# Routing steps with lower bound and step width side by side in one tile, one summing instruction and two moving instructions per step

## The chip, the cores and the metric

The kernel runs on one core of one Trainium2 chip. Its metric is device time in microseconds (us). Five engines work side by side, each through its own queue in order: PE (TensorE, matmuls; PEld is its weight load), DVE (VectorE), ACT (ScalarE), POOL (GpSimd) and SP, which here only issues DMAs. They wait for one another through semaphores. SBUF is the working memory, PSUM holds eight banks into which matmuls write.

## What is computed

The reference chains three blocks: attention over a local band and block summaries, a dense feed-forward block with a gate, and a mixture of eight experts in which every token goes to exactly one expert. The third is the one that matters here:

```python
def _moe2_ref(x, w_gate, w1, w2):
    N, D = x.shape                      # 1536, 512
    E = w_gate.shape[1]                 # 8
    cap = N // E                        # 192
    logits = x @ w_gate
    order = np.argsort(-logits.flatten())
    assigned = -np.ones(N); counts = np.zeros(E)
    for idx in order:
        tok, e = idx // E, idx % E
        if assigned[tok] >= 0 or counts[e] >= cap:
            continue
        assigned[tok] = e; counts[e] += 1
    for e in range(E):
        mask = assigned == e
        out[mask] = np.maximum(x[mask] @ w1[e], 0.0) @ w2[e]
```

The greedy loop means: each expert has a lower bound on the logit that it still takes, and the eight bounds have to be such that each expert ends with exactly 192 tokens.

## The kernel before

Attention and the first product of the feed-forward block (`gemm1`) come first, then the second product (`gemm2`), then the experts. Between `gemm1` and the experts the tokens have to be assigned. The kernel does this while `gemm2` runs: the function `drive` takes the two generators (`second`, which is `gemm2`, and `routing`) and interleaves them by fixed weights, so that the order of instructions on each queue is settled when the program is written. On PE this gives, per routing step, one batch of 12 small matmuls of the routing (L894) and then 18 matmuls of `gemm2` (L704 to L706), and then the next batch.

`route` finds the eight bounds in 15 steps (and a 16th that only makes the assignment). Logits of all tokens lie as 128 partitions x 12 x 8. The bounds `lo` and step widths `step` are 8 numbers each, the same on all partitions. One step does this on DVE, unless PE is named:

- L870 to L882: which logits are below the bound, each token's best expert among those left (`prop`), and beside these small instructions on 8 columns: L873 and L874 make 1/`step`, L878 makes `lo - step`.
- L885, L887, L889: for each token the number of step widths by which its logit lies above the bound, and the comparison of it with 16 thresholds at once (`C`, 128 x 1536 in 16 bits; in the profile its name is `big`).
- L894, on PE: 12 matmuls with a matrix of ones count the tokens per expert and threshold into PSUM.
- L897, L899: the count is compared with the capacity, and each hit is multiplied by a table entry (`dG` for the bound, `dU` for the width); L901 and L903 sum each of these over the 16 thresholds.
- L904, L906: the bound moves by sum times `step`; L908: the width becomes (1 + sum) times `step`.

`lo` lies in SBUF. `step`, its successor `step2`, the product `inc`, the logits' copy `Lp`, `Lm` and `u` lie in one PSUM bank (`state`). The semaphore waits among DVE's own instructions go by whole tiles: one that reads this bank waits for the last one that wrote it, whichever part that was.

During the steps ACT and POOL prepare operands for `gemm2`: ACT rounds a slice (L681), POOL forms the remainder (L682, both inputs and the output in SBUF); they do two slices per routing step, and their start is set by the `gemm2` matmuls on PE that release their buffers.

Of the kernel before, what the change touches and what calls it, by code (L numbers as in the profile page):

```python
# [7 lines left out]
FT = mybir.dt.float32  # L8
# [4 lines left out]
OP = mybir.AluOpType  # L13
AX = mybir.AxisListType
# [8 lines left out]
E, EF = 8, 1024  # L23
N = B * S
CAP = N // E
NT = N // 128
# [14 lines left out]
J = 16  # L41
# [41 lines left out]
def attention_moe_moe(tc, q, k, v, w_in, w_out, w_gate, w1, w2, out):  # L83
    with ExitStack() as ctx:
        build(ctx, tc, q, k, v, w_in, w_out, w_gate, w1, w2, out)


def build(ctx, tc, q, k, v, w_in, w_out, w_gate, w1, w2, out):
    nc = tc.nc
    PE, ACT, DVE, POOL, SP = nc.tensor, nc.scalar, nc.vector, nc.gpsimd, nc.sync  # L90
# [28 lines left out]
    def bank(i):  # L119
        return psum.tile([128, 512], FT, name=f"bank{i}")  # L120
# [658 lines left out]
    for u in range(NU):  # L779
# [5 lines left out]
        else:  # L785
# [4 lines left out]
            big = late.tile([128, 2 * 2 * 512], I32)  # L790
# [16 lines left out]
    def last_sums():  # L807
        while taken[0] < NF:
            out_slice()
            yield 2000  # L810
        for g in range(NF // FG, NF // FG + 2):
            fold_pair(g)
            yield 900
        routing_constants()
        for u in range(NU):
            yield from logits(u)
        summed.append(1)
# [1 line left out]

    prop = late.tile([128, NT, E], F16)  # L820
    jc, C = [big[:, i * 768:(i + 1) * 768].bitcast(F16).rearrange("p (j c) -> p j c", j=J) for i in range(2)]
    dG, dU = [big[:, 1536 + i * E * J:1536 + (i + 1) * E * J].bitcast(FT).rearrange("p (e j) -> p e j", e=E)
              for i in range(2)]
    ones = big[:, 1792:1792 + 64].bitcast(F16)
    g = [0.0] + [RATIO ** i for i in range(J - 1)]
    upd = [1.0] + [(b - a) / g[-1] * SPREAD for a, b in zip(g, g[1:])] + [GROW]

    def routing_constants():
        POOL.memset(ones, 1.0)
        for j in range(J):  # L830
            DVE.memset(jc[:, j, :], 0.5 if j == 0 else g[j] + 1.0)
            DVE.memset(dG[:, :, j], 0.0 if j == 0 else g[j] - g[j - 1])
            DVE.memset(dU[:, :, j], upd[j + 1] - upd[j])

    okf = late.tile([128, 1], FT)
    slot = late.tile([128, NT], I32)
# [1 line left out]
    def small(name, shape, dt=FT):  # L838
        return late.tile(shape, dt, name=name, bufs=2)

    def bc(x):
        return x[:, None, :].to_broadcast([128, NT, E])

    def route():
        mm = small("mm", [128, 2, E])
        Le = L.rearrange("p t e -> p e t")
        DVE.tensor_reduce(mm[:, 0], Le, axis=AX.X, op=OP.max)
        DVE.tensor_reduce(mm[:, 1], Le, axis=AX.X, op=OP.min)
        DVE.tensor_scalar(mm[:, 1], mm[:, 1], -1.0, None, op0=OP.mult)
        yield 100  # L850
        p = bank(7)
        PE.transpose(p[:2 * E, :128], mm.rearrange("p a e -> p (a e)"), ident)
        mc = small("mc", [2 * E, 1])
        DVE.tensor_reduce(mc, p[:2 * E, :128], axis=AX.X, op=OP.max)
        yield 100
        p = bank(7)
        PE.matmul(p[:, :2 * E], mc.to_broadcast([2 * E, 128]), ident[:2 * E, :2 * E], start=True, stop=True)
        state = bank(4)
        Lp, Lm, u = [state[:, i * NT * E:(i + 1) * NT * E].rearrange("p (t e) -> p t e", t=NT) for i in range(3)]
        step, inc, step2 = [state[:, 3 * NT * E + i * E:3 * NT * E + (i + 1) * E] for i in range(3)]  # L860
        DVE.tensor_copy(Lp, L)
        lo = small("lo", [128, E])
        DVE.tensor_scalar(lo, p[:, E:2 * E], -1.0, None, op0=OP.mult)
        DVE.tensor_tensor(step, p[:, :E], lo, op=OP.subtract)
        DVE.tensor_scalar(step, step, 1.0 / g[-1], 1e-30, op0=OP.mult, op1=OP.max)
        for n in range(STEPS):
            last = n == STEPS - 1
            below = small("Lm", [128, NT, E])
            pm = small("pm", [128, NT])
            DVE.tensor_tensor(below, Lp, bc(lo), op=OP.is_lt)  # L870
            if not last:
                inv = small("inv", [128, E])
                DVE.tensor_scalar(inv, step, 1e-30, None, op0=OP.max)  # L873
                DVE.reciprocal(inv, inv)  # L874
            DVE.scalar_tensor_tensor(Lm, below, -BIG, Lp, op0=OP.mult, op1=OP.add)
            if not last:
                l1 = small("l1", [128, E])
                DVE.tensor_tensor(l1, lo, step, op=OP.subtract)  # L878
            DVE.tensor_reduce(pm, Lm, axis=AX.X, op=OP.max)
            if not last:  # L880
                DVE.tensor_tensor(u, Lp, bc(l1), op=OP.subtract)
            DVE.tensor_tensor(prop, Lm, pm[:, :, None].to_broadcast([128, NT, E]), op=OP.is_equal)  # L882
            if last:
                return
            DVE.scalar_tensor_tensor(u, u, 0.0, bc(inv), op0=OP.max, op1=OP.mult)  # L885
            w = small("w", [128, NT * E], F16)
            DVE.scalar_tensor_tensor(w, u.rearrange("p t e -> p (t e)"), 6e4, prop.rearrange("p t e -> p (t e)"),  # L887
                                     op0=OP.min, op1=OP.mult)
            DVE.tensor_tensor(C, w[:, None, :].to_broadcast([128, J, NT * E]), jc, op=OP.is_ge)  # L889
            yield 100  # L890
            p = bank(7)
            Cv = C.rearrange("p j (t e) -> p j t e", e=E)
            for t in range(NT):
                PE.matmul(p[:, :J * E], ones, Cv[:, :, t, :], start=t == 0, stop=t == NT - 1)  # L894
            cnt = p[:, :J * E].rearrange("p (j e) -> p e j", e=E)
            ge = small("ge", [128, E, J])
            DVE.scalar_tensor_tensor(ge, cnt, CAP - 0.5, dG, op0=OP.is_ge, op1=OP.mult)  # L897
            gu = small("gu", [128, E, J])
            DVE.scalar_tensor_tensor(gu, cnt, CAP - 0.5, dU, op0=OP.is_ge, op1=OP.mult)  # L899
            gain = small("inc", [128, E])  # L900
            DVE.tensor_reduce(gain, ge, axis=AX.X, op=OP.add)  # L901
            up = small("up", [128, E])
            DVE.tensor_reduce(up, gu, axis=AX.X, op=OP.add)  # L903
            DVE.tensor_tensor(inc, gain, step, op=OP.mult)  # L904
            lo2 = small("lo", [128, E])
            DVE.tensor_tensor(lo2, lo, inc, op=OP.add)  # L906
            lo = lo2
            DVE.scalar_tensor_tensor(step2, up, 1.0, step, op0=OP.add, op1=OP.mult)  # L908
            step, step2 = step2, step

    tok = late.tile([128, NT], FT)
    POOL.iota(tok, pattern=[[128, NT]], base=0, channel_multiplier=1, allow_small_or_imprecise_dtypes=True)
# [32 lines left out]
    def routing():  # L945
        while not summed:
            yield 50
        yield from route()
        yield 100
        place(prop, True)  # L950
        placed[0] = 1
        POOL.iota(at, pattern=[[1, CAP]], base=0, channel_multiplier=0, allow_small_or_imprecise_dtypes=True)
        DVE.tensor_copy(lslot, slot[:, NT - 1:])
        DVE.tensor_scalar(hot, at, lslot, None, op0=OP.is_equal)
# [267 lines left out]
```

## Time and profile before

| | us |
|---|---|
| median of 3 runs | 597.47 (595.98 to 600.57) |
| the profiled execution, its own time | 597.21 |
| its span, first to last instruction | 595.4 |
| PE busy | 554.4 (93%) |
| DVE busy | 384.4 (65%) |
| ACT busy | 288.7 (48%) |
| POOL busy | 170.2 (29%) |

The mean granted TensorE clock is 0.971 of full speed. The busy share is an average over stages: attention and `gemm1` fill the first 296 us, the routing steps lie between 307 and 394 us beside `gemm2`, and the experts run from 430 us on. The part of the page that cuts the span in 40 slices shows PE at eight to nine tenths in the slices of the routing steps.

### The profile page before, as it was taken

The numbers are of one execution on the slowest core, as the hardware profiler recorded it, in microseconds if no ns is written. First come the engines' busy times: TensorE is split into PE (matmuls) and PEld (weight loads), VectorE is DVE, ScalarE is ACT, GpSimd is POOL, SyncE is SP. The second block draws the span as 40 slices with busy tenths as digits, with TensorE's granted clock in tenths as the row PEclk, the third lists the DMA queues.
The fourth block names the chain that finished last, engine by engine and source line by source line (L and its number), as shares of the span: only waits on it lengthen the run. The fifth ranks groups of instructions, "written<-read, shape, count | busy, mean of one in ns | idle before, by whom it ended". The sixth has DMA issues, their size and how long they took to land.

```text
span 595.4 us, 10943 instructions
## 1 busy us (share of the span) xinstructions
PE 554.4 (93%) x3811; PEld 469.4 (79%) x3811; DVE 384.4 (65%) x1215; ACT 288.7 (48%) x694; POOL 170.2 (29%) x204
## 2 busy tenths in 40 slices
PE   7769889989999999999999899899999999999994
PEld 6647778878899989976677667678789888988883
DVE  6787985655534397731037787762588888888880
ACT  4265654435645445651131131133577777776760
POOL 1424448211111024562243344445101101110011
PEclk9688899989999999999999999999999999999997
DMA  9974991202220245420070000003579878878811
GB/s 207 245 193 101 236 275 35 53 18 62 52 48 1 70 146 175 143 64 1 1 211 2 0 2 1 0 33 129 175 224 282 238 242 272 270 230 270 246 59 32
DMA packets 102400, 75.06 MB, mean 126 GB/s; under 512 B 47488, under 2 KB 88448, under 8 KB 101952
## 3 DMA queue, kind: packets, MB, share of 16 engines
q1 hardware_dynamic: 100352, 67.96, 41.4%
q0 software_dynamic: 1984, 6.32, 2.9%
q8 instruction: 32, 0.52, 0.4%
q14 instruction: 32, 0.26, 0.2%
HBM read 67.55 MB, written 6.71 MB: 125 GB/s over the span
## 4 chain that ended last, share of the span: by engine, by line
PE 43%; issue 26%; DVE 18%; DMA 5%; POOL 3%; ACT 2%; SPq 1%; POOLq 0%; DVEq 0%; ACTq 0%
PE bank L587 7%; PE bank L588 6%; PE bank L589 6%; PE bank L704 4%; PE bank L705 3%; PE bank L706 3%; DVE big L889 3%; POOL out_dram L1025 2%; PE bank L894 2%; DVE bank L268 2%; PE bank L419 2%; PE bank L613 2%; DMA t<-in_moe_w_in_dram 2%; DMA t<-in_q_dram 2%; PE bank L372 2%
## 5 line engine op out<-in xcount | busy, mean ns | idle before, releaser
L587 PE MATMUL bank<-x,wh 128*128 128x384 f32 x256 | 92.5, 361 | 6.6 <-DVE t L601 5.1
L295 DVE TENSOR_TENSOR wl<-t,wh 128x1024 fp32r<-128x1024 f32 x64 | 77.0, 1220 | 20.5 <-ACT wh L294 18.7
L681 ACT ACTIVATE work<-t 128x384 fp32r<-128x384 f32 (+2 forms) x80 | 36.4, 459 | 106.2 <-PE bank L705 101.9
L588 PE MATMUL bank<-x,wh 128*128 128x384 f32 x256 | 87.0, 340 | 0.6 <-DVE x L77 0.6
L589 PE MATMUL bank<-x,wl 128*128 128x384 f32 x256 | 87.2, 340 | 0.1
L590 ACT ACTIVATE t<-bank,three 128x384 f32<-128x384 f32 x64 | 37.2, 581 | 93.8 <-PE bank L589 93.7
L682 POOL TENSOR_TENSOR tlx<-t,work 128x384 fp32r<-128x384 f32 (+1 forms) x52 | 55.8, 1074 | 83.4 <-ACT work L681 83.4
L704 PE MATMUL bank<-wh,work 128*128 128x512 f32 x192 | 78.1, 407 | 0.0
L706 PE MATMUL bank<-wh,tlx 128*128 128x512 f32 x192 | 75.3, 392 | 0.1
L705 PE MATMUL bank<-wl,work 128*128 128x512 f32 x192 | 74.8, 390 | 0.0
L1050 PE MATMUL bank<-x,wh 128*128 128x384 f32 x256 | 73.7, 360 | 0.5 <-DVE x L976 0.5
L294 ACT ACTIVATE wh<-t 128x1024 fp32r<-128x1024 f32 x64 | 65.6, 1048 | 0.0
L1052 PE MATMUL bank<-x,wl 128*128 128x192 f32 x256 | 64.2, 251 | 0.0
L601 DVE SCALAR_TENSOR_TENSOR t<-t,bank 128x384 f32<-128x384 f32 x64 | 34.9, 549 | 39.7 <-ACT t L590 39.6
L396 POOL TENSOR_TENSOR A<-A,sm 128x480 f32<-128x480 f32 x24 | 23.7, 987 | 124.2 <-ACT at L406 72.6
L587 PEld LDWEIGHTS bank<-x,wh 128*128 128x128 f32 x256 | 48.7, 190 | 11.5 <-DVE t L601 4.3
L1025 POOL DMA_INDIRECT out_dram<-t,idx x16 | 14.9, 929 | 141.6 <-DVE t L1074 136.1
L588 PEld LDWEIGHTS bank<-x,wh 128*128 128x128 f32 x256 | 48.9, 191 | 1.2 <-DVE x L77 1.1
L589 PEld LDWEIGHTS bank<-x,wl 128*128 128x128 f32 x256 | 48.8, 191 | 0.5 <-POOL wl L286 0.5
L1052 PEld LDWEIGHTS bank<-x,wl 128*128 128x128 f32 x256 | 48.9, 191 | 0.3
L1066 PE MATMUL bank<-wh,t 128*128 128x512 f32 x128 | 49.0, 392 | 0.0
L1050 PEld LDWEIGHTS bank<-x,wh 128*128 128x128 f32 x256 | 48.0, 188 | 1.2 <-DVE x L976 0.8
(184 smaller groups left out, 1072.0 us busy)
## 6 DMA issues: line engine op xcount, KB each, us to landing
t<-in_moe_w_dram SPq DMA_DIRECT2D x128, 256.0 KB
t<-in_moe_w_in_dram SPq DMA_DIRECT2D x16, 512.0 KB
big<-in_moe_w_out_dram SPq DMA_DIRECT2D x16, 512.0 KB
VW<-in_v_dram SPq DMA_DIRECT2D x20, 192.0 KB
t<-in_v_dram SPq DMA_DIRECT2D x4, 768.0 KB
t<-xs SPq DMA_DIRECT2D x8, 258.0 KB
raw<-in_q_dram SPq DMA_DIRECT2D x8, 256.0 KB
t<-in_k_dram SPq DMA_DIRECT2D x12, 128.0 KB
```

The costliest lines, as they stand in the source:

```text
L294: ACT.activation(hi, x, AF.Copy)
L295: DVE.tensor_tensor(lo, x, hi.bitcast(FT), op=OP.subtract)
L587: PE.matmul(p, wh[:, kk, :], xh[:, kk, :], start=kk == 0, stop=False)
L588: PE.matmul(p, wh[:, kk, :], xl[:, kk, :], start=False, stop=False)
L589: PE.matmul(p, wl[:, kk, :], xh[:, kk, :], start=False, stop=kk == KD - 1)
L682: (DVE if placed[0] else POOL).tensor_tensor(ths[i][1], t, ths[i][0].bitcast(FT), op=OP.subtract)
L704: PE.matmul(acc[j], th[:, c], WH[s], start=f == 0, stop=False)
L705: PE.matmul(acc[j], th[:, c], WL[s], start=False, stop=False)
L706: PE.matmul(acc[j], tl[:, c], WH[s], start=False, stop=f == NF - 1)
L1050: PE.matmul(p, a[:, kk, :], xt[:, kk].rearrange("p c s -> p (c s)"), start=kk == 0, stop=False, skip_group_check=True)
L1052: PE.matmul(p[:, :CAP], b[:, kk, :], xt[:, kk, 0, :], start=False, stop=kk == KD - 1, skip_group_check=True)
L1066: PE.matmul(p, x, w, start=m == 0 and i == 0, stop=m == NM - 1 and i == 2)
```

## The change

`lo` and `step` become the two halves of one SBUF tile `ls` (128 x 2 x 8). The tables `dG` and `dU` become one table `dGU`, the two sets of hits one tile `hit` (128 x 2 x 8 x 16). Both comparisons stay, but one TENSOR_REDUCE sums both sets (128 x 256 to 128 x 16, into the PSUM bank), one multiplication by `step` makes both moves and one addition makes the new pair of bound and width. So L901 and L903 become one instruction, and L904, L906, L908 become two; a step has 16 DVE instructions where it had 18.

```diff
-    dG, dU = [big[:, 1536 + i * E * J:1536 + (i + 1) * E * J].bitcast(FT).rearrange("p (e j) -> p e j", e=E)
-              for i in range(2)]
+    dGU = big[:, 1536:1536 + 2 * E * J].bitcast(FT).rearrange("p (a e j) -> p a e j", a=2, e=E)
...
-        step, inc, step2 = [state[:, 3 * NT * E + i * E:3 * NT * E + (i + 1) * E] for i in range(3)]
+        gains, moves = [state[:, 3 * NT * E + i * 2 * E:3 * NT * E + (i + 1) * 2 * E].rearrange("p (a e) -> p a e", a=2)
+                        for i in range(2)]
         DVE.tensor_copy(Lp, L)
-        lo = small("lo", [128, E])
+        ls = small("lo", [128, 2, E])
+        lo, step = ls[:, 0], ls[:, 1]
...
-            ge = small("ge", [128, E, J])
-            DVE.scalar_tensor_tensor(ge, cnt, CAP - 0.5, dG, op0=OP.is_ge, op1=OP.mult)
-            gu = small("gu", [128, E, J])
-            DVE.scalar_tensor_tensor(gu, cnt, CAP - 0.5, dU, op0=OP.is_ge, op1=OP.mult)
-            gain = small("inc", [128, E])
-            DVE.tensor_reduce(gain, ge, axis=AX.X, op=OP.add)
-            up = small("up", [128, E])
-            DVE.tensor_reduce(up, gu, axis=AX.X, op=OP.add)
-            DVE.tensor_tensor(inc, gain, step, op=OP.mult)
-            lo2 = small("lo", [128, E])
-            DVE.tensor_tensor(lo2, lo, inc, op=OP.add)
-            lo = lo2
-            DVE.scalar_tensor_tensor(step2, up, 1.0, step, op0=OP.add, op1=OP.mult)
-            step, step2 = step2, step
+            hit = small("ge", [128, 2, E, J])
+            for i in range(2):
+                DVE.scalar_tensor_tensor(hit[:, i], cnt, CAP - 0.5, dGU[:, i], op0=OP.is_ge, op1=OP.mult)
+            DVE.tensor_reduce(gains, hit, axis=AX.X, op=OP.add)
+            DVE.tensor_tensor(moves, gains, step[:, None].to_broadcast([128, 2, E]), op=OP.mult)
+            ls2 = small("lo", [128, 2, E])
+            DVE.tensor_tensor(ls2, moves, ls, op=OP.add)
+            ls, lo, step = ls2, ls2[:, 0], ls2[:, 1]
```

With the shorter text all later lines of `route` count otherwise: what is L870 before is L871 after, L873 is L874, L874 is L875, L875 is L876, L878 is L879, L879 is L880, L881 is L882, L889 is L890, L894 is L895.

The end of a step on DVE, before (bank_3296 holds the counts, bank_3250 is `state`, `inc` in the first TENSOR_REDUCE is the tile of `gain`; a bracket says that the instruction waits for an earlier one of DVE or for PE):

```order
L897 SCALAR_TENSOR_TENSOR ge<-bank_3296,big 128x128 [waits PE_49]
L899 SCALAR_TENSOR_TENSOR gu<-bank_3296,big 128x128
L901 TENSOR_REDUCE inc<-ge 128x8 [waits DVE_49]
L903 TENSOR_REDUCE up<-gu 128x8 [waits DVE_49]
L904 TENSOR_TENSOR bank_3250<-inc,bank_3250 128x8 [waits DVE_49]
L906 TENSOR_TENSOR lo<-lo,bank_3250 128x8 [waits DVE_49]
L908 SCALAR_TENSOR_TENSOR bank_3250<-up,bank_3250 128x8 [waits DVE_49]
```

The same place after the change:

```order
L899 SCALAR_TENSOR_TENSOR ge<-bank_3296,big 128x128 [waits PE_49]
L899 SCALAR_TENSOR_TENSOR ge<-bank_3296,big 128x128
L900 TENSOR_REDUCE bank_3250<-ge 128x16 [waits DVE_49]
L901 TENSOR_TENSOR bank_3250<-bank_3250,lo 128x16 [waits DVE_49]
L903 TENSOR_TENSOR lo<-bank_3250,lo 128x16 [waits DVE_49]
```

Two sums and three moves have become one sum and two moves, each of which needs the one just in front of it.

The start of the following step on DVE, before (`l_3328` is `lo - step`):

```order
L870 TENSOR_TENSOR Lm<-bank_3250,lo 128x96 [waits DVE_49]
L873 TENSOR_SCALAR inv<-bank_3250 128x8
L874 RECIPROCAL inv<-inv 128x8 [waits DVE_49]
L875 SCALAR_TENSOR_TENSOR bank_3250<-Lm,bank_3250 128x96
L878 TENSOR_TENSOR l_3328<-lo,bank_3250 128x8 [waits DVE_49]
L879 TENSOR_REDUCE pm<-bank_3250 128x12
L881 TENSOR_TENSOR bank_3250<-bank_3250,l_3328 128x96 [waits DVE_49]
```

The same place after the change:

```order
L871 TENSOR_TENSOR Lm<-bank_3250,lo 128x96 [waits DVE_49]
L874 TENSOR_SCALAR inv<-lo 128x8
L875 RECIPROCAL inv<-inv 128x8 [waits DVE_49]
L876 SCALAR_TENSOR_TENSOR bank_3250<-Lm,bank_3250 128x96
L879 TENSOR_TENSOR l_3323<-lo 128x8
L880 TENSOR_REDUCE pm<-bank_3250 128x12 [waits DVE_49]
L882 TENSOR_TENSOR bank_3250<-bank_3250,l_3323 128x96 [waits DVE_49]
```

The instructions are the same, but L874 and L879 read the tile `lo` in SBUF where their forerunners read the PSUM bank (L879 reads it twice), and the wait that stood at the subtraction now stands at the TENSOR_REDUCE behind it. The order on PE, ACT, POOL and SP is the same as before.

## Rows read from the trace of the kernel before

**Rows 1.** What PE waited for, 300 to 420 us: total, times, longest.

```profile
PE bank L894 <- DVE big L889: 8.2, 15, 0.6
```

**Rows 2.** The same view, 395 us to the end.

```profile
PE bank L1050 <- DVE x L976: 0.5, 1, 0.5
```

**Rows 3.** Timeline, PE: start us, duration, engine, line, operation; idle before.

```profile
312.09 0.84 PE L894 MATMUL bank<-big 128*128 128x128 f16 x12 [0.31 <-DVE big L889]
...
312.75 0.48 PE L704 MATMUL bank<-wh,work 128*128 128x512 f32 x1
...
316.72 0.39 PE L706 MATMUL bank<-wh,tlx 128*128 128x512 f32 x1
...
317.68 0.84 PE L894 MATMUL bank<-big 128*128 128x128 f16 x12 [0.58 <-DVE big L889]
```

**Rows 4.** The chain that ended last: two of its 15 count batches.

```profile
357.20 0.86 PE bank L894 x12
...
385.15 0.86 PE bank L894 x12
```

**Rows 5.** Timeline, DVE, one step.

```profile
358.08 0.29 DVE L897 SCALAR_TENSOR_TENSOR ge<-bank,big 128x128 f32<-128x128 f32 x1 [0.94 <-PE bank L894]
358.29 0.28 DVE L899 SCALAR_TENSOR_TENSOR gu<-bank,big 128x128 f32<-128x128 f32 x1
...
358.68 0.28 DVE L903 TENSOR_REDUCE up<-gu 128x8 f32<-128x128 f32 x1
...
359.26 0.17 DVE L908 SCALAR_TENSOR_TENSOR bank<-up,bank 128x8 f32<-128x8 f32 x1
359.46 0.26 DVE L870 TENSOR_TENSOR Lm<-bank,lo 128x96 f32<-128x96 f32 x1
359.64 0.16 DVE L873 TENSOR_SCALAR inv<-bank 128x8 f32<-128x8 f32 x1
359.83 0.20 DVE L874 RECIPROCAL inv<-inv 128x8 f32<-128x8 f32 x1
359.95 0.24 DVE L875 SCALAR_TENSOR_TENSOR bank<-Lm,bank 128x96 f32<-128x96 f32 x1
360.23 0.16 DVE L878 TENSOR_TENSOR l<-lo,bank 128x8 f32<-128x8 f32 x1
360.31 0.25 DVE L879 TENSOR_REDUCE pm<-bank 128x12 f32<-128x96 f32 x1
...
361.77 0.96 DVE L889 TENSOR_TENSOR big<-w,big 128x1536 f16<-128x1536 f16 x1
```

**Rows 6.** Groups by line and shape: busy us, mean ns.

```profile
L309 DVE TENSOR_REDUCE ks<-kT 128x16 f32<-128x512 f32 x6 | 4.1, 684 | 2.4 <-ACT kT L308 2.3
```

**Rows 7.** Timeline, POOL, during the routing steps.

```profile
310.21 1.01 POOL L682 TENSOR_TENSOR tlx<-t,work 128x384 fp32r<-128x384 f32 x1 [1.58 <-ACT work L681]
...
315.54 1.01 POOL L682 TENSOR_TENSOR tlx<-t,work 128x384 fp32r<-128x384 f32 x1 [2.27 <-ACT work L681]
...
359.94 1.01 POOL L682 TENSOR_TENSOR tlx<-t,work 128x384 fp32r<-128x384 f32 x1 [1.95 <-ACT work L681]
361.99 1.59 POOL L682 TENSOR_TENSOR tlx<-t,work 128x384 fp32r<-128x384 f32 x1 [1.04 <-ACT work L681]
...
387.80 0.74 POOL L682 TENSOR_TENSOR tlx<-t,work 128x256 fp32r<-128x256 f32 x1 [1.85 <-ACT work L681]
```

**Rows 8.** Timeline, DVE, the two longest comparisons of the 15.

```profile
310.50 1.54 DVE L889 TENSOR_TENSOR big<-w,big 128x1536 f16<-128x1536 f16 x1
...
350.20 1.34 DVE L889 TENSOR_TENSOR big<-w,big 128x1536 f16<-128x1536 f16 x1
```

**Rows 9.** One line of the attention part: ns min/median/max.

```profile
L382 DVE TENSOR_SCALAR sm<-sm x24: 169/276/1100, 11.1 to 189.9; 128x4 f32<-128x4 f32 x24
```

**Rows 10.** Timeline, POOL and DVE, one of these.

```profile
189.19 0.99 POOL L396 TENSOR_TENSOR A<-A,sm 128x480 f32<-128x480 f32 x1 [6.82 <-ACT at L406]
...
189.89 0.31 DVE L382 TENSOR_SCALAR sm<-sm 128x4 f32<-128x4 f32 x1
```

More of the change, by code (lines that the diff above doesn't have):

```diff
@@ L831, in routing_constants @@
             DVE.memset(jc[:, j, :], 0.5 if j == 0 else g[j] + 1.0)
-            DVE.memset(dG[:, :, j], 0.0 if j == 0 else g[j] - g[j - 1])
-            DVE.memset(dU[:, :, j], upd[j + 1] - upd[j])
+            DVE.memset(dGU[:, 0, :, j], 0.0 if j == 0 else g[j] - g[j - 1])
+            DVE.memset(dGU[:, 1, :, j], upd[j + 1] - upd[j])
     okf = late.tile([128, 1], FT)
```

## The prediction, made before the changed kernel was timed

> **What bounds the kernel now.** I read the waits of PE first, since PE is busy for 93% of the span. During the routing steps PE waits for one thing: 15 times the count batch L894 waits for the comparison L889 on DVE, 8.2 us in all [rows 1]. Behind them PE waits once more, 0.5 us [rows 2]; what the routing steps gain or lose is carried to the end almost whole. Next, the timeline of PE. Of the 18 `gemm2` matmuls of a step the first starts at 312.75 and the last at 316.72, 17 intervals of 0.234; the 18th is through at 316.95, but the batch starts at 317.68 [rows 3]. So DVE's chain sets the pace, and PE would let it be 0.73 us faster per step and no more. The period is 5.59 us: (385.15 - 357.20) / 5 [rows 4].
>
> Then DVE's own pace, from one step [rows 5]. An instruction without a wait starts about 0.08 us before the one ahead ends: L873 at 359.64, while L870 lasts to 359.72; L875 and L879 likewise. One that waits for its neighbour starts 0.03 to 0.04 after its end: L874 at 359.83, L873 ended at 359.80. A wait on the neighbour thus costs 0.11 us. The 7 instructions at the end of a step alternate between two independent pairs, and take 358.08 to 359.46, 1.38 us.
>
> Last, POOL. Its L682 (SBUF in, SBUF out) and DVE hold each other up. L889 reads two SBUF tensors; it takes 0.96 us [rows 5], but 1.54 when it started at 310.50 behind a POOL instruction that ran from 310.21 to 311.22 [rows 7, 8]: it ended 0.82 after POOL, as if only its first 0.13 had passed. The other way round POOL started at 361.99 behind L889 (361.77 to 362.73) and took 1.59 in place of 1.01, ending 0.85 after DVE: 0.16 had passed [rows 5, 7]. Size is no shelter: L382, 4 columns from SBUF to SBUF, takes 0.17 when free and up to 1.10 [rows 9]; one ended at 190.20, 0.02 after POOL's 190.18 [rows 10]. While POOL ran from 359.94 to 360.95, L878 and L879 (one input in PSUM) kept their durations [rows 5].
>
> **The change, part by part.** Tables, first values and the order on the other engines cost nothing that PE sees.
>
> End of a step. The comparisons stay, 0.21 apart, the second ends at 0.49. The sum must wait for it: 0.52. Its length is the unknown one. For 128 columns the row has 0.28 [rows 5], for 512 columns 0.684 [rows 6]; the line between them gives 0.41 for 256. Bounds: 0.28 (as now) and 0.56 (two of now); I take 0.41, since both neighbours have this operation and type. Then two moves of 16 columns in a row, each 0.03 of wait and 0.17 (8 columns take 0.16 to 0.17): 0.96, 1.16, and the next step begins at 1.36. So two instructions fewer give only 0.02 us: what is left is a chain in which each waits for its neighbour.
>
> Start of the next step. The subtraction (L878, L879 after) no longer waits for L875 and may start at 0.16 behind it, in place of 0.28; the TENSOR_REDUCE behind it now waits for L875 itself and starts at 0.27 in place of 0.36: 0.09 us. Free of POOL a step gains 0.11 us.
>
> But the subtraction now reads two SBUF tensors, like L889, and the first half of the reciprocal (L874) reads and writes SBUF, like L382. In the step that I show, counted from the batch at 357.20, the subtraction would start at 359.93 + 0.16 = 360.09 and need its second input at 360.22; POOL starts at 359.94 and holds from 360.10 [rows 7]. POOL is first by 0.12. The subtraction ends at about 360.98, the reduction starts at 360.90 in place of 360.20: 0.70 late. The comparison follows the reduction by 1.46 (361.77 - 360.31) [rows 5]: 362.36. Now POOL's second instruction, at 361.99, is ahead of it, so the roles change: POOL runs free to 363.00, the comparison ends 0.83 later at 363.83 in place of 362.73. **The step is 1.10 us longer.** POOL's own times are set by PE's matmuls counted from the batch, so the next step looks alike.
>
> Which steps? Ahead of the second to seventh comparison POOL is late: in the step from 312.09 the subtraction would be over by 315.14, and POOL starts at 315.54 [rows 3, 7]: 6 steps gain 0.11, together 0.66. The first comparison (310.50) and the eighth (350.20) were held by POOL already [rows 8] and end when they did: 0. The ninth to fourteenth follow batches like that at 357.20: 6 x 1.10 = 6.60. The fifteenth follows 385.15 with a shorter POOL instruction, 387.80 to 388.54 [rows 4, 7]: the subtraction due at 388.04 ends at 388.57, the reduction is 0.34 late, the comparison would start at 389.95. POOL's second, 2.05 behind its first as above, is at 389.85, still ahead, and lasts 0.74: the comparison ends at 391.42 in place of 390.69, 0.73 more.
>
> Sum: -0.66 + 6.60 + 0.73 = +6.7 us. The profiled execution took 597.21, 0.26 below the median of the runs (597.47); I put the sum on it: **603.9 us**.
>
> No row shows a DVE instruction of 8 FP32 columns and two SBUF inputs beside POOL; the nearest is L889 (the same operation, two SBUF inputs, 16 bits), and in the other direction those with one PSUM input, which are never held. I take L889. The Trainium skill ("SBUF — State Buffer", "SBUF: two separate sides") says that a DVE instruction with two SBUF inputs, of whatever size, shares a port pair with a POOL instruction that reads SBUF, and that whichever starts first holds it for the whole of its run; by it the sum is the one above, without it the 595.8 of the first rival.
>
> **The rivals.**
>
> *No hold: faster, though not by much.* Either 8 FP32 columns are not held, or DVE wins the race. The point that decides is a start of the subtraction near 359.97 in the step shown; a sum of 0.28 us in place of 0.41 would bring it to 359.96. For it: a margin of only 0.12 us, built from six terms. Against: every term has a row but that one. Then 13 steps gain 0.11 (the two held by POOL gain nothing): -1.4, 595.8; with a sum of 0.28, 0.24 a step, 594.1; with 0.56 it loses 0.04 a step, 597.7. Chance 0.24.
>
> *One hold only.* The comparison escapes POOL's second instruction: a held step loses 0.59, the last 0.23, the sum is +3.1, 600.3. Against it: 362.36 is 0.37 behind POOL's start. Chance 0.07.
>
> *Every instruction saved counts.* Two starts 0.195 apart (358.29 to 358.68 are two) saved in 13 steps: -5.1, 592.1. Against it: the waits on neighbours in the order after the change, 0.11 each. The Trainium skill ("VectorE: DVE Perf Modes", "The DRAIN you can't avoid") has a kindred rule: an instruction starts only when the one ahead has drained, and waits cost nothing extra. As durations added up that is 1.62 now, with L903 and L878 standing for their like, and 1.32 after, 0.30 in 13 steps, 593.3. The row speaks against the rule: the 7 take 1.38, not 1.62. Chance 0.03.
>
> *More than this.* POOL also catches other steps, or PE, idle for a quarter of a held step, gets a lower clock: above 605.5. Chance 0.05. And the width is now step + sum x step, rounded otherwise than (1 + sum) x step; should the bounds miss 192 anywhere, the exact assignment and the experts run again, some 165 us more at the least: 0.01.
>
> **How the numbers follow.** My forecast, two holds in seven steps, has 0.60. Its own range is 602.5 to 605.5: the sum's length moves the six free steps by -0.8 to +0.9, and the held ones by little. The range of all, 594.8 to 605.5, takes in the three likeliest cases up to their thin ends and leaves out some 0.15. One per cent, about what can be told from no change, is 6.0 us: from 603.4 on it is slower. The forecast lies only 0.5 above that, so two thirds of it, 0.40, and the 0.06 above are slower: 0.46. Within one per cent are the rest of it (0.20), the free case and the single hold: 0.51. Every instruction saved lies at the edge (592.1, and one per cent down is 591.5); I count its 0.03 as faster.
>
> **What would show it.** In the timeline of DVE: the TENSOR_REDUCE L900 at about 0.41 us; 1.36 us from the first comparison L899 to L871; L879 at 0.16 us in early steps and at about 0.9 from the batch near 351 us on, ending right behind POOL's L682; the comparison L890 at 0.96 early, about 1.47 late; POOL's second L682 down from 1.59 to 1.01; PE's wait for it up from 8.2 us to some 15. If L879 stays at 0.16 throughout, the first rival holds. If L900 is far from 0.41, the race is decided there.

## The result, and the profile after

| | before | after |
|---|---|---|
| median of ten runs each (us) | 597.4 (594.56 to 600.57) | 603.5 (598.4 to 607.23) |
| ratio to before, 95% interval | | 1.0113 (1.0084 to 1.0143) |
| the profiled execution, its own time | 597.21 | 598.40 |
| its span | 595.4 | 596.5 |
| first to last of the 15 count batches | 78.65 | 85.53 |

The change costs some 6 us, against +6.7 forecast. But the profiled execution of after is the shortest of its ten, only 1.2 above that of before. The chain of waits shows where the difference of the two lies (start us, us, what):

```profile
306.46 0.86 PE bank L895 x12
...
352.37 0.86 PE bank L895 x12
...
365.69 0.86 PE bank L895 x12
...
391.99 0.84 PE bank L895 x12
```

The first count batch comes at 306.46; before it came at 312.09 [rows 3]. The work ahead of the routing is the same but for the layout of two tables and the place of the first width, and from the first bound on the same time passes in both: 4.59 us from L863 (before, 307.50) and L864 (after, 301.87) to the first batch. The other kernels here, with nearly that same work, differ as much ahead of the first batch (last section), so I don't count these 5.63 us as the change's. From there to the last batch after takes 85.53 us, 6.88 more; behind it 204.5 us are left, before 204.7. So -5.63 + 6.88 - 0.15 = +1.1, the difference of the spans. The windows of the first 50 us (us, busy and instructions of PE, PEld, DVE, ACT, POOL, granted clock, DMA share, GB/s), of before and then of after, differ in the granted clock (0.80 and 0.90):

```profile
0.00:50.00 50.00, 35.92 (x353) 29.34 (x354) 38.42 (x151) 23.90 (x79) 17.41 (x24) 0.80 0.89 204
```

```profile
0.00:50.00 50.00, 36.48 (x385) 29.27 (x386) 40.19 (x156) 26.96 (x91) 18.46 (x25) 0.90 0.97 218
```

From 300 to 430 us the granted clock is 1.00 in both, so it has no part in what follows. From here on I read each kernel by the intervals between its count batches, which within one execution mostly repeat to 0.02 us, and take the runs' times second.

What PE waited for from 300 to 420 us (total, times, longest), to be set beside [rows 1]:

```profile
PE bank L895 <- DVE big L890: 15.0, 15, 1.7
```

and from 395 us to the end, beside [rows 2]:

```profile
PE bank L1045 <- DVE x L971: 0.5, 1, 0.5
```

PE's wait for the comparison went from 8.2 to 15.0 us, and nothing behind gave it back. The lines of the subtraction and the comparison (ns min/median/max, first and last start, forms):

```profile
L879 DVE TENSOR_TENSOR l<-lo x15: 153/157/865, 303.6 to 388.6; 128x8 f32<-128x8 f32 x15
L890 DVE TENSOR_TENSOR big<-w,big x15: 957/1386/1457, 305.2 to 390.5; 128x1536 f16<-128x1536 f16 x15
```

The same instruction on 8 columns takes 153 ns in one step and 865 in another. In the timeline of DVE, a free early step, beside [rows 5]:

```profile
329.52 0.49 DVE L899 SCALAR_TENSOR_TENSOR ge<-bank,big 128x128 f32<-128x128 f32 x2 [0.94 <-PE bank L895]
330.05 0.43 DVE L900 TENSOR_REDUCE bank<-ge 128x16 f32<-128x256 f32 x1
330.51 0.18 DVE L901 TENSOR_TENSOR bank<-bank,lo 128x16 f32<-128x16 f32 x1
330.73 0.17 DVE L903 TENSOR_TENSOR lo<-bank,lo 128x16 f32<-128x16 f32 x1
330.93 0.26 DVE L871 TENSOR_TENSOR Lm<-bank,lo 128x96 f32<-128x96 f32 x1
...
331.57 0.15 DVE L879 TENSOR_TENSOR l<-lo 128x8 f32<-128x8 f32 x1
331.70 0.26 DVE L880 TENSOR_REDUCE pm<-bank 128x12 f32<-128x96 f32 x1
```

A late one, with POOL's two instructions and the count batch:

```profile
355.12 1.01 POOL L682 TENSOR_TENSOR tlx<-t,work 128x384 fp32r<-128x384 f32 x1 [3.63 <-ACT work L681]
355.15 0.24 DVE L876 SCALAR_TENSOR_TENSOR bank<-Lm,bank 128x96 f32<-128x96 f32 x1
355.30 0.86 DVE L879 TENSOR_TENSOR l<-lo 128x8 f32<-128x8 f32 x1
356.08 0.24 DVE L880 TENSOR_REDUCE pm<-bank 128x12 f32<-128x96 f32 x1
...
357.16 0.99 POOL L682 TENSOR_TENSOR tlx<-t,work 128x384 fp32r<-128x384 f32 x1 [1.03 <-ACT work L681]
...
357.54 1.43 DVE L890 TENSOR_TENSOR big<-w,big 128x1536 f16<-128x1536 f16 x1
359.02 0.84 PE L895 MATMUL bank<-big 128*128 128x128 f16 x12 [1.66 <-DVE big L890]
```

The subtraction starts 0.18 behind POOL's first instruction and ends at 356.16, 0.03 behind that one's end (356.13). L876, with one of its inputs in PSUM, starts between the two and keeps its 0.24. The comparison, late now, starts 0.38 behind POOL's second instruction and ends 0.82 behind its end (358.15). POOL's second takes 0.99, where it took 1.59 behind the comparison [rows 7].

Intervals between count batches, in us, of all kernels that ran (differences of starts in the chain of waits, one execution each). The early six follow the first batch, the late six the eighth. I call the subtraction held where POOL stretches it beyond its free 0.16, and a step held where its subtraction is:

| kernel | early six | 7th | late six | last | first to last batch |
|---|---|---|---|---|---|
| before | 5.59 | 5.97 | 5.58 to 5.60 | 5.59 | 78.65 |
| after | 5.54 to 5.56 | 5.98 | 6.65 to 6.67 | 6.31 | 85.53 |
| sub_early | 5.55 | 5.98 | 5.54 to 5.55 | 5.55 | 78.12 |
| sub_mid | 5.59 to 5.60 | 5.99 | 5.59 to 5.60 | 6.30 | 79.42 |
| step_sbuf | 5.32 to 5.34 | 5.98 | 5.31 to 5.33 | 6.30 | 76.18 |
| step_sbuf_sub_early | 5.32 to 5.33 | 5.98 | 5.32 to 5.33 | 5.32 | 75.21 |
| two_sums_sub_early | 5.47 | 5.98 | 5.47 | 5.47 | 77.09 |
| no_pool | 5.40 to 5.55 | 5.69 | 5.41 to 5.55 | 5.55 | 77.52 |
| first_pool_only | 5.57 to 5.63 | 6.03 | 5.54 to 5.56 | 5.56 | 78.56 |
| first_pool_sub_late | 5.62 to 5.63 | 6.03 | five 6.31 to 6.32, one 5.63 | 5.94 | 82.94 |
| before_sub_early | 5.52 to 5.53 | 5.99 | 5.51 to 5.53 | 5.52 | 77.77 |

### The profile page after: what moved, and what is told of

It is laid out like the page before. It is cut to its first block, busy times and chain, and to the rows that moved or that the text cites. A ratio compares the mean times of both kernels' runs of the same rounds, so it can differ in the third digit from the quotient of the medians.

```text
span 596.5 us, 10913 instructions
## 1 busy us (share of the span) xinstructions
PE 549.6 (92%) x3811; PEld 465.1 (78%) x3811; DVE 392.0 (66%) x1185; ACT 288.6 (48%) x694; POOL 166.7 (28%) x204
## 3 DMA queue, kind: packets, MB, share of 16 engines
q0 software_dynamic: 1984, 6.32, 2.9%
## 4 chain that ended last, share of the span: by engine, by line
PE 37%; issue 26%; DVE 20%; DMA 6%; POOL 6%; ACT 2%; SPq 1%; POOLq 0%; DVEq 0%; ACTq 0%
PE bank L587 6%; PE bank L588 5%; PE bank L589 5%; PE bank L704 4%; PE bank L705 3%; PE bank L706 3%; DVE big L890 3%; POOL out_dram L1020 2%; PE bank L895 2%; DVE bank L268 2%; PE bank L613 2%; DMA t<-in_moe_w_in_dram 2%; POOL t L186 2%; DMA t<-in_q_dram 2%; DMA big<-in_moe_w_out_dram 1%
## 5 line engine op out<-in xcount | busy, mean ns | idle before, releaser
L682 POOL TENSOR_TENSOR tlx<-t,work 128x384 fp32r<-128x384 f32 (+1 forms) x52 | 51.5, 992 | 93.8 <-ACT work L681 93.8
```

The source lines that it names most:

```text
L682: (DVE if placed[0] else POOL).tensor_tensor(ths[i][1], t, ths[i][0].bitcast(FT), op=OP.subtract)
```

## The experiments

The four with an interval ran against one set of runs of before (median 596.95 of 35). Their ratios lie up to 0.2% below the quotients of the medians, so these small gains in the runs' times are known no better than that. The others are single executions, read by their intervals between batches.

**sub_early: the change, with the subtraction ahead of POOL's start.**

```diff
             DVE.tensor_scalar(inv, step, 1e-30, None, op0=OP.max)
+            l1 = small("l1", [128, E])
+            DVE.tensor_tensor(l1, lo, step, op=OP.subtract)
             DVE.reciprocal(inv, inv)
         DVE.scalar_tensor_tensor(Lm, below, -BIG, Lp, op0=OP.mult, op1=OP.add)
-        if not last:
-            l1 = small("l1", [128, E])
-            DVE.tensor_tensor(l1, lo, step, op=OP.subtract)
```

> The changed kernel with the subtraction lo - step moved between the two halves of the reciprocal; nothing else. Theory (POOL holds the subtraction, and that delays the comparison into POOL's second instruction): it then starts about 0.35 us ahead of POOL's L682, is never held (0.16 us throughout, not 0.86), the comparison is 0.96 us except in the first and eighth step, and first to last count batch takes 13 x 5.54 + 5.98 = 78.0 us (85.5 in the changed kernel, 78.65 in the one before): about 596.5 us. Rival (the serial chain of sum and moves is what costs): the stage stays at some 85 us and the time at about 603.

Measured: 596.54 us (593.14 to 600.3), ratio to before 0.9972 (0.9943 to 1.0). No step is held; the stage takes 78.12, against 78.0 expected. Its timeline of DVE and POOL in a late step:

```profile
354.51 0.16 DVE L876 TENSOR_TENSOR l<-lo 128x8 f32<-128x8 f32 x1
354.72 1.01 POOL L682 TENSOR_TENSOR tlx<-t,work 128x384 fp32r<-128x384 f32 x1 [1.95 <-ACT work L681]
356.50 0.96 DVE L889 TENSOR_TENSOR big<-w,big 128x1536 f16<-128x1536 f16 x1
356.79 1.52 POOL L682 TENSOR_TENSOR tlx<-t,work 128x384 fp32r<-128x384 f32 x1 [1.05 <-ACT work L681]
```

Same instructions, same operands, same POOL: only the place of one instruction of 8 columns differs, and 7.4 us of the stage (85.53 - 78.12) are gone. POOL's second is the long one again.

**no_pool: the change, without POOL's instructions.** During the routing steps the remainders of `gemm2`'s operands are left out (its matmuls read the rounded slice in their place), so POOL's L682 is gone there.

```diff
-                (DVE if placed[0] else POOL).tensor_tensor(ths[i][1], t, ths[i][0].bitcast(FT), op=OP.subtract)
+                if routed_on[0]:
+                    ths[i] = ths[i][0], ths[i][0]
+                else:
+                    (DVE if placed[0] else POOL).tensor_tensor(ths[i][1], t, ths[i][0].bitcast(FT), op=OP.subtract)
```

> The changed kernel in which POOL's remainders for gemm2 (L682) are left out during the routing steps; the matmuls that would read them read the rounded slice instead, so the order and number of matmuls stay. Theory (POOL is what holds the two DVE instructions): the subtraction 0.16 and the comparison 0.96 in all steps but perhaps the first, stage 14 x 5.54 = 77.6 us. Rival (the slower steps come from DVE's own chain, the PSUM bank or ACT): the seven long steps stay at 6.66, stage 85.5.

Measured: stage 77.52, one execution 594.77. In its timeline of DVE the subtraction is at its old place and free, and in its groups by line (busy us, mean ns) the 15 comparisons are at their free length:

```profile
357.93 0.16 DVE L883 TENSOR_TENSOR l<-lo 128x8 f32<-128x8 f32 x1
...
359.53 0.96 DVE L895 TENSOR_TENSOR big<-w,big 128x1536 f16<-128x1536 f16 x1
```

```profile
L895 DVE TENSOR_TENSOR big<-w,big 128x1536 f16<-128x1536 f16 x15 | 14.4, 958 | 0.6
```

So it takes both: the place behind POOL's start, and POOL's instruction.

**step_sbuf: before, with the step width alone moved to SBUF.** The edit of the change that brings the hold, without the common sum and moves.

```diff
-        step, inc, step2 = [state[...] for i in range(3)]
+        inc = state[:, 3 * NT * E:3 * NT * E + E]
+        step = small("step", [128, E])
...
+            step2 = small("step", [128, E])
             DVE.scalar_tensor_tensor(step2, up, 1.0, step, op0=OP.add, op1=OP.mult)
-            step, step2 = step2, step
+            step = step2
```

> The kernel before with only the step width moved from the PSUM bank to an SBUF tile; two sums and three moves as before. The subtraction and two of the moves then read two SBUF tensors. Waits on the bank fall away: the end of a step should take 1.18 us (1.38 before), and the subtraction start 2.71 us after the count batch; POOL's first instruction starts at 2.75 in the later steps. By the race as read from the rows (DVE needs its second input 0.13 after its start, POOL its port 0.16 after) DVE is just ahead: no hold, a step of about 5.3 us, stage 75.1 us, about 593.9 us. Rival (an instruction with two SBUF inputs is held whenever POOL runs at any time of it, or the placing in SBUF alone is what costs): held in seven steps as in the changed kernel, stage about 82 us, about 601.

Measured: 596.02 us (593.35 to 599.14), ratio 0.9969 (0.9939 to 0.9999); stage 76.18. The free steps of 5.33 are as expected, the six late ones among them. The last one is held, which I had not expected. Timeline of DVE and POOL, a late step and the last:

```profile
354.21 0.15 DVE L879 TENSOR_TENSOR l<-lo,step 128x8 f32<-128x8 f32 x1
354.25 1.01 POOL L682 TENSOR_TENSOR tlx<-t,work 128x384 fp32r<-128x384 f32 x1 [1.95 <-ACT work L681]
...
386.08 0.74 POOL L682 TENSOR_TENSOR tlx<-t,work 128x256 fp32r<-128x256 f32 x1 [1.85 <-ACT work L681]
386.14 0.70 DVE L879 TENSOR_TENSOR l<-lo,step 128x8 f32<-128x8 f32 x1
```

0.04 ahead of POOL the subtraction is free, 0.06 behind it is held to POOL's end. The edit gains 0.26 in a free step (5.59 to 5.33): with the width out of the bank fewer instructions wait for a neighbour.

**step_sbuf_sub_early: both edits above on before.** The diffs are those of step_sbuf and sub_early together.

> The same with the subtraction moved between the two halves of the reciprocal, so that it is over 0.3 us before POOL starts. Theory: end of a step 1.18 us, start of the next 0.77 (0.85 before), a step of 5.3 us, stage 78.65 - 13 x 0.28 = 75.0 us, 593.8 us: faster than both kernels. Rival (PE cannot take count batches earlier, or instructions with two SBUF inputs are slower in themselves): 597 or more.

Measured: 594.73 us (590.41 to 597.44), ratio 0.9947 (0.9918 to 0.9976), stage 75.21, 3.44 below before: faster than both kernels, with the 18 DVE instructions a step that before has. Its timeline of DVE, the end of a late step and the start of the next:

```profile
354.11 0.29 DVE L897 SCALAR_TENSOR_TENSOR ge<-bank,big 128x128 f32<-128x128 f32 x1 [0.94 <-PE bank L894]
...
355.18 0.16 DVE L909 SCALAR_TENSOR_TENSOR step<-up,step 128x8 f32<-128x8 f32 x1
355.30 0.26 DVE L871 TENSOR_TENSOR Lm<-bank,lo 128x96 f32<-128x96 f32 x1
```

The free steps are those of step_sbuf (5.32 to 5.33); what the early subtraction adds is the last step, 6.30 there and 5.32 here. The end of a step takes 1.19 us (354.11 to 355.30), with two sums and three moves; after takes 1.41 for one sum and two moves.

**two_sums_sub_early: sub_early, with the sum split in two again**, and its result in an SBUF tile in place of the PSUM bank.

```diff
-            DVE.tensor_reduce(gains, hit, axis=AX.X, op=OP.add)
+            gains = small("inc", [128, 2, E])
+            for i in range(2):
+                DVE.tensor_reduce(gains[:, i], hit[:, i], axis=AX.X, op=OP.add)
```

> The changed kernel with two TENSOR_REDUCE of 128 columns (into an SBUF tile) in place of one of 256, and the subtraction early. Theory: the long sum buys nothing, since the move must wait for all of it: end of a step 1.34 us with two short sums against 1.41 with one, start 0.77; a step 5.47, stage 77.1 us, 595.8 us. Rival (fewer instructions are faster): slower than the run with one sum and the subtraction early, stage above 78.0.

Measured: 594.63 us (591.06 to 597.98), ratio 0.9956 (0.9926 to 0.9986), stage 77.09. One instruction more than sub_early, and 0.08 us less a step. In its timeline of DVE:

```profile
334.22 0.49 DVE L897 SCALAR_TENSOR_TENSOR ge<-bank,big 128x128 f32<-128x128 f32 x2 [0.94 <-PE bank L893]
334.62 0.47 DVE L900 TENSOR_REDUCE inc<-ge 128x8 f32<-128x128 f32 x2
335.12 0.18 DVE L901 TENSOR_TENSOR bank<-inc,lo 128x16 f32<-128x16 f32 x1
```

The first sum starts 0.40 behind the first comparison, before the second is through (0.49), though both comparisons write one SBUF tile: here the first sum doesn't wait for the tile's last writer. The moves start at 0.90. In after the sum waits for both comparisons (0.53) and the moves start at 0.99. What the other place of the result adds to this wasn't tried by itself.

**sub_mid: the change, with the subtraction one place earlier** (the two lines of sub_early behind the reciprocal), to put it close to POOL's start.

> The changed kernel with the subtraction moved by one place, ahead of L876 and behind the reciprocal, so that in the later steps it starts some 0.03 us behind POOL's first instruction in place of 0.18. By the rows the point that decides lies at about that distance (POOL needs the port 0.16 after its start, DVE 0.13 after its own): if the race goes by these points the result is one or the other as a whole, held in all seven steps (stage about 85) or in none (about 78.0). Rival (whoever starts first by the record wins): held in all seven.

Measured: stage 79.42, one execution 598.05. Timeline of DVE and POOL, a late step and the last:

```profile
354.15 1.03 POOL L682 TENSOR_TENSOR tlx<-t,work 128x384 fp32r<-128x384 f32 x1 [1.96 <-ACT work L681]
354.18 0.12 DVE L877 TENSOR_TENSOR l<-lo 128x8 f32<-128x8 f32 x1
...
387.61 0.73 POOL L682 TENSOR_TENSOR tlx<-t,work 128x256 fp32r<-128x256 f32 x1 [1.85 <-ACT work L681]
387.75 0.62 DVE L877 TENSOR_TENSOR l<-lo 128x8 f32<-128x8 f32 x1
```

0.02 to 0.03 behind POOL's start it is still free, in all six late steps; 0.14 behind it is held. I had expected all or none, and it is neither: the last step's distance is another. Two things differ from the other runs and keep the deciding point vague: at this place the free subtraction takes 0.12, not 0.16, so its recorded start may mark a somewhat later moment, and POOL's instruction in the last step is the shorter one of 256 columns.

**first_pool_only: the change, with only the first of POOL's two instructions.** As no_pool, but under the condition `routed_on[0] and i % 2`: every second remainder is left out.

> The changed kernel in which only every second of POOL's remainders is left out during the routing steps, the one that stands ahead of the comparison in the later steps. Theory of two holds: the subtraction is still held (0.86), the comparison no longer (0.96), a held step takes 5.54 + 0.70 = 6.2 us in place of 6.66, stage 14 x 5.54 + 6 x 0.70 + 0.3 = 82.1 us. Rival (one hold makes all of the delay): 85.5; rival (the hold of the comparison is the only one that counts): 77.6.

Measured: stage 78.56, one execution 599.17, no subtraction held. A miss: the edit moved what I meant to keep. Timeline of DVE and POOL, a late step:

```profile
356.49 0.15 DVE L883 TENSOR_TENSOR l<-lo 128x8 f32<-128x8 f32 x1
356.62 1.01 POOL L685 TENSOR_TENSOR tlx<-t,work 128x384 fp32r<-128x384 f32 x1 [3.92 <-ACT work L681]
```

POOL's remaining instruction starts 0.13 behind the subtraction, so there was no race to lose, and what one hold costs stayed open.

**first_pool_sub_late: the same, with the subtraction one place later** (behind the TENSOR_REDUCE of `pm`), so that POOL is first again.

> Every second of POOL's remainders is left out during the routing steps, and the subtraction stands behind the TENSOR_REDUCE L880, one place later than in the changed kernel, so that it meets POOL's one instruction in the later steps (it would start some 0.17 us behind it). Theory: held once, to POOL's end; the instruction behind it is 0.77 us late, and as POOL has no second instruction the comparison stays at 0.96: steps of about 6.3 us late, 5.65 early, stage about 84 us. Rival (the first hold is made up for by the time of the comparison, and only the comparison's own hold delays PE): stage below 80 us.

Measured: stage 82.94, one execution 598.29. Five late steps are held at 6.31 to 6.32, one is free at 5.63, and the last is held (5.94). Timeline, a held step and the free one:

```profile
364.03 1.01 POOL L685 TENSOR_TENSOR tlx<-t,work 128x384 fp32r<-128x384 f32 x1 [5.30 <-ACT work L681]
...
364.21 0.85 DVE L884 TENSOR_TENSOR l<-lo 128x8 f32<-128x8 f32 x1
...
366.29 0.96 DVE L895 TENSOR_TENSOR big<-w,big 128x1536 f16<-128x1536 f16 x1
...
383.17 0.16 DVE L884 TENSOR_TENSOR l<-lo 128x8 f32<-128x8 f32 x1
```

In the free step POOL started at 383.27, 0.10 behind the subtraction. With no second POOL instruction the comparison keeps 0.96, and the hold costs 6.32 - 5.63 = 0.69 us. After, with both, loses 6.66 - 5.55 = 1.11: the second hold adds 0.42.

**before_sub_early: before, with the subtraction moved as in sub_early.** It reads PSUM here, so POOL plays no part.

> The kernel before with nothing but the subtraction moved between the two halves of the reciprocal (it reads the PSUM bank there as before). Theory: the wait on the neighbour falls away, 0.08 us a step, stage 13 x 5.51 + 5.98 = 77.6 us, nothing held that was free before. Rival (the wait is not what sets the start of the next instruction): 78.65 as before.

Measured: stage 77.77; a step takes 5.52 in place of 5.59. The instructions are the same; the move alone is worth 0.07.

## Why the prediction came true, step by step

**PE's slack and the rest.** Every kernel here stays within the 0.73 us per step that PE would allow; the fastest step, 5.32, uses 0.27 of it. What the routing stage lost reached the end whole.

**The hold.** Right in mechanism and size. The subtraction was put at 0.15 behind POOL and 0.89 long, and it was 0.18 and 0.86; the comparison 1.47, and it was 1.43; POOL's second 1.01, and it was 0.99; PE's wait some 15, and it was 15.0. A held step lost 1.07 against before (6.66 - 5.59; 1.10 forecast), the last 0.72 (0.73). In the 7th interval the subtraction was free and the comparison held by POOL as before (1.39 at 344.26, before 1.34 [rows 8]); it moved by 0.01, as put. sub_early and no_pool take away place and partner in turn, and either removes all of it. With one input in PSUM the same subtraction was never held: in before it starts 0.28 behind POOL in the late steps and takes 0.16 [rows 5, 7].

**The free steps: the term that was off.** Forecast -0.11 each, -0.66 in all; measured -0.03 to -0.05, -0.27 in all. The start of a step is as put: 330.93 to 331.70 is 0.77, before 0.85, so 0.08 (0.09 put). The end of a step is not: 1.41 in place of 1.36, where 1.38 had been before. The sum took 0.43 (0.41 put), and the gaps and the 16-column moves made up the rest. Two instructions fewer per step cost 0.03 us there instead of saving 0.02.

**The sum.** -0.27 + 0.01 + 6.42 + 0.72 = +6.88 in the stage; forecast -0.66 + 0 + 6.60 + 0.73 = +6.67. Part of this closeness is luck: the free steps gained 0.39 less than put and the held ones lost 0.18 less, and the two misses partly offset. The medians differ by 6.1, the interval of the ratio is +5.0 to +8.5 us; that the median came within 0.4 of the forecast says no more than that.

**The rivals.** *No hold* named the right point of decision but the wrong side of it. By start of the two-SBUF subtraction against POOL's start, over all runs: free at every distance up to +0.03 (-0.13, -0.04 and +0.03 among them); held at +0.06, +0.14, +0.17 to +0.19 and, in the last step of after and of first_pool_sub_late, +0.29. The forecast put the point at 0.03 and the subtraction at 0.15. The rows thus differ from the Trainium skill ("SBUF — State Buffer", "SBUF: two separate sides") in one thing: by it whichever starts first holds, while at +0.03 the one that starts later by the record still got through (in sub_mid, where the recorded start may be late by that much). In the rest the rows above agree with it: two SBUF inputs were held, one input in PSUM was not, and the one held ended behind the other. *One hold only* falls with the 1.43 us of the comparison. *Every instruction saved counts* falls twice: after's end of a step is longer with two instructions fewer, and two_sums_sub_early is faster with one more (though its sums also go to SBUF). Its kindred rule in the Trainium skill ("VectorE: DVE Perf Modes", "The DRAIN you can't avoid": a semaphore cost nothing extra in the copies measured there) doesn't hold here either: before_sub_early moves one instruction into a wait and gains 0.07 us a step. *More than this* didn't come: no early step was held, and the granted clock stayed at 1.00 through the held steps.

## What to carry to other kernels

Before an operand of a small DVE instruction is moved from PSUM to SBUF, look in the timeline at which POOL instructions run beside it and which starts first: 8 columns were enough to lose 0.7 us, and the delay brought a second loss further on. Count the waits on the neighbour, not the instructions: merging two independent pairs into one chain gained nothing, while taking the width out of the bank, and waits with it, gained 0.26 us a step (step_sbuf), and moving an independent instruction into a wait 0.07 (before_sub_early). The second gain isn't general: on step_sbuf and on after the same move left the free steps as they were (5.33 and 5.55) and only took away the holds. And where executions differ by more than the effect, compare a stage from its first to its last event: here the stage showed 0.5 us (78.65 and 78.12), where the times of twelve runs left an interval of 3 us.

## What was not expected of the hardware

- A race is not decided by the recorded start alone: DVE won when 0.03 us behind POOL and lost at 0.06, though in two kernels and beside POOL instructions of 384 and 256 columns.
- One SBUF input can be enough. The scaling of the first width reads and writes one tile, and with that tile in SBUF it is held too, 0.29 us behind POOL's start (301.98); in before, with the width in PSUM, it takes 0.17 at the same distance (307.91, POOL 307.62), and 0.17 in no_pool, which has no POOL instruction there. The first comparison, held by POOL in both kernels, hides this loss, so the forecast that the first values cost nothing came true for a reason that it didn't name. Timeline of DVE, after:

```profile
302.27 0.75 DVE L866 TENSOR_SCALAR lo<-lo 128x8 f32<-128x8 f32 x1
```

- POOL is held by DVE for small instructions as well. A COPY of 3 columns took 0.18 in before, but 0.92 in after, where it started (391.06) inside the held comparison of the last step (390.48 to 391.94). Timeline of POOL, after:

```profile
391.06 0.92 POOL L725 COPY x<-tok 128x3 f32<-128x3 f32 x1
```

- Most of the spread between the profiled executions arises ahead of the routing: with nearly the same instructions the first count batch came at 306.46 us in one (after) and at 315.29 in another (step_sbuf_sub_early), with a granted clock in the first 50 us of 0.90 and 0.80. Behind the last batch all eleven took 204.5 to 205.2 us. The clock isn't all of it: at 0.86 it came at 311.46 in two_sums_sub_early and at 313.85 in first_pool_only. What else sets it stays open.
